# State and output products of an attention tile gathered around the next tile's transposes and scores

## The chip, the cores and the metric

The kernel runs on one core of a Trainium2 chip. The metric is the device time of one execution in microseconds (us); three executions of the kernel before took 817.29 to 818.46 us, with a median of 818.1 us. In the text PE is the matrix engine (TensorE), DVE the vector engine, ACT the scalar engine, POOL the GpSimd engine, SP the queue engine that issues transfers. PEld is the loading of weights into PE.

## The reference

Three layers follow each other on 3072 tokens (4 batches of 768, 384 features):

```python
for t in range(S):                      # linear attention, 8 heads of 48, decay w
    cur = einsum('bhd,bhe->bhde', u[None] * kt, vt)
    y[:, :, t] = einsum('bhd,bhde->bhe', rt, state + cur)
    state = wt[:, :, :, None] * state + einsum('bhd,bhe->bhde', kt, vt)
x = y.transpose(0, 2, 1, 3).reshape(B * S, H * D)
h = x @ w_in                            # dense layer, 384 -> 2048 -> 384
x = (max(h, 0) + alpha * min(h, 0)) @ w_out
expert_idx = argmax(cosine(x, expert_emb) / tau)
out = gate * (relu(x @ w1[expert_idx]) @ w2[expert_idx])   # one of 8 experts, 384 -> 1024 -> 384
```

All is in float32.

## The kernel before, in words

**Attention** is cut into 24 tiles: six chunks of 128 steps in time for each of four batches (`n // 4` is the chunk, `n % 4` the batch). A tile's loaded data (`ld`, 1348.5 KB, two buffers) is worked on in parts that the code calls by a digit and a letter for the engine. The parts that matter here:

- 0D and 1D (lines 277 to 290): two scans on DVE that turn the decays into running products, and products with k. 6D (line 302): r times the running product on DVE, and the old state scaled into `sbd` on POOL. 7D: the term with `u` (a reduction and a product on DVE, giving `dv`). 8A: a check of the decays on ACT.
- 2P, 2A: k is transposed on PE (`kt_ps`, four products, L341) and copied by ACT into the single buffer `Kt`.
- 3P, 3A: the scores of all eight heads (`a_ps`, two PSUM tiles, eight products that the trace shows as 16 matmuls, L352), copied by ACT into the single buffer `A` and masked by POOL.
- 9P, 9A: the new part of the state, `Kt` times v (`u_ps`, L368), added to `sbd` on DVE (L376). It is called from inside 4P and 4D.
- 4P, 4D: the output y of the tile, from the old state (L391) and from the scores (L394) into `y_ps`, then `dv` is added on DVE (L400).
- 5P, 5A, 5D: y is transposed (`t_ps`, L409) and split into `xh` and `xl`, the input of the dense layer.

The matrices that PE uses differ in shape: `kt`, `t` and all products of the dense layer use the whole array (128*128 in the trace), the scores use half of its rows (64*128), the state and y use half of its columns (128*64; `u` shows 48 of 64 active).

**The dense layer** works on blocks of three tiles (`BLK`, eight blocks, 384 tokens). Block j has 16 steps `f`; step T = 16 j + f computes `l1` (nine products into `h_ps`, L453; ACT, DVE, ACT and DVE then make `gh` and `gl` from it) and `l2` of the step two before (nine products into three `o_ps`, L488). Every value is split into a high and a low part, hence three products for one. After a block, `route` finds each token's expert with some 60 small DVE operations, a few of them after each step.

**The order** is written out by hand. For the first block it is the string `PLAN`; from then on the table `sched` gives for each step T the parts of tiles that run in it. Parts 2 to 5 come at a step's start (before `l1` on PE), parts 0, 1, 6, 8, 9 and 7 at its end (after `l2`). For a tile n of block q the start is `16 * (q - 1) + AT[3][n - B0[q]]`, and `LAGS` says how many steps later each part comes:

```python
LAGS = [0, 1, 4, 4, 6, 7, 2]
AT = {2: [-1, 6], 3: [-4, 1, 7]}
```

So a tile's transposes and scores stand together at one step, its state and y two steps later, its transposed y one step after that: three groups on PE for each tile, each between the `l2` of one step and the `l1` of the next. `run` (line 942) also issues the load of tile n + 2 when every part that reads tile n is recorded. PSUM holds three `o` buffers, two `h` buffers and three `a` buffers; `a` is shared by `kt_ps`, both `a_ps`, `u_ps`, `y_ps`, `t_ps` and a small product of `route`.

**The expert layer** follows from about 557 us on; its weights are loaded by index and its order is another table.

Of the kernel before, what the change touches and what calls it, by code (L numbers as in the profile page):

```python
# [8 lines left out]
F32 = mybir.dt.float32  # L9
# [8 lines left out]
B, H, S, D = 4, 8, 768, 48  # L18
# [3 lines left out]
NCH = S // CH  # L22
NTILE = B * NCH
HP = H // 2
# [6 lines left out]
BLK = [3] * 8  # L31
NB = len(BLK)
B0 = [sum(BLK[:j]) for j in range(NB)]
# [25 lines left out]
STEP7 = 5  # L59
# [12 lines left out]
START = [-8, -6, -5]  # L72
LAGS0 = [0, 1, 2, 2, 3, 4, 1]
LAGS1 = [0, 1, 4, 4, 6, 7, 2]
LAGS = [0, 1, 4, 4, 6, 7, 2]

LOADS = [(0, "w"), (0, "rk"), "id", "v", (0, "n"), "e", (1, "w"), (1, "rk"), (1, "n"), (2, "w"), (2, "rk"), (2, "n"), 0, 1, 2, 3, "u"]
PLAN = """
# [11 lines left out]
m.15 p1P.6 p1A.6 4P.5 4D.5 o.12 5P.5 5A.5 d.14 p0P.7 o.13 p0A.7 c2.15 5D.5 p1P.7 c3.15 n.15 p1A.7  # L90
"""

AT1 = {1: [0, 4, 8], 2: [0, 4, 8]}
AT = {2: [-1, 6], 3: [-4, 1, 7]}
NSG = 4
WP = 1536
W_MID = 0.95
# [9 lines left out]
def tile_main(ctx, tc, keep, x2d, tbl, att, w_in, w_out, alpha, u_row, u_col, emb, tau, w1, w2, cst, out):  # L107
# [13 lines left out]
    ps_h = ctx.enter_context(tc.tile_pool(name="ps_h", bufs=2, space=bass.MemoryType.PSUM))  # L121
    ps_a = ctx.enter_context(tc.tile_pool(name="ps_a", bufs=3, space=bass.MemoryType.PSUM))
# [57 lines left out]
    def rT(n, i):  # L180
        return ld_t[n][:, i * HP * CH:(i + 1) * HP * CH].rearrange("p (h t) -> p h t", h=HP)

    def nat(n, i):
        return ld_t[n][:, LN + i * DM:LN + (i + 1) * DM]
# [43 lines left out]
    wt_t, tmp = {}, {}  # L228
# [132 lines left out]

    def att_9P(n):
        v = nat(n, 2)
        up = tmp["u", n] = ps_a.tile([128, HP, D], F32, tag="a", name="u_ps")
        for h in range(H):
            i = h % 2
            q = slice(64 * i, 64 * i + D)
            PE.matmul(out=up[q, h // 2, :], lhsT=Kt[:, h // 2, q], rhs=v[:, D * h:D * h + D], start=True, stop=True)  # L368
# [11 lines left out]
    def att_4P(n):  # L380
        c, b = divmod(n, B)
        r, v = rT(n, 0), nat(n, 2)
        A = tmp.pop(("A", n))
        if 0 < c < NCH - 1:
            att_9P(n)
        yp = tmp["y", n] = ps_o.tile([128, DM], F32, tag="o", name="y_ps") if n < BT else ps_a.tile([128, DM], F32, tag="a", name="y_ps")

        for hp in range(HP):
            for q in (slice(0, 64), slice(64, 128)):
                if c:  # L390
                    PE.matmul(out=yp[q, 2 * D * hp:2 * D * (hp + 1)], lhsT=r[:, hp, q], rhs=sbd[n % 2][:, hp, :], start=(hp == 0), stop=False)  # L391
            for h in (2 * hp, 2 * hp + 1):
                for q in (slice(0, 64), slice(64, 128)):
                    PE.matmul(out=yp[q, D * h:D * h + D], lhsT=A[:, HP * (h % 2) + h // 2, q], rhs=v[:, D * h:D * h + D], start=(c == 0 and h == 0), stop=(h == H - 1))  # L394
# [31 lines left out]
    def parts(q, n):  # L426
        if q == 2 and n // B == NCH - 1 or q == 9 and n > BT:
            return []
        if q == 7:
            return [p for p in PART[7] if n in ND and (p != "7D" or n not in AD) or n not in ND and p == "7D"]  # L430
        return PART[q]
# [423 lines left out]
    if True:  # L855
# [40 lines left out]
        for n in range(B0[NB - 1], NTILE):  # L896
            c, b = divmod(n, B)
            t0 = b * S + c * CH
            SP.dma_start(out=x2d[t0:t0 + CH, :], in_=sbd_all.rearrange("p i h d -> p (i h d)")[:, 0:ROW])


        sched = {}
        for n in range(NTILE):
            j = max(q for q in range(NB) if B0[q] <= n)
            t0 = START[n] if j == 0 else 16 * (j - 1) + (AT1[j] if j < 3 else AT[BLK[j]])[n - B0[j]]
            for q, d in enumerate(LAGS0 if j == 0 else LAGS1 if j == 1 else LAGS):
                sched.setdefault(t0 + d, []).append((q, n))
            sched.setdefault({1: 0, 2: 1}.get(n, t0 + 3), []).append((8, n))
        sched.setdefault(1, []).append((2, 2))
# [3 lines left out]
        ran = set()  # L913
# [25 lines left out]
        def run(name, *a):  # L939
            if name == "w":  # L940
                return warm(*a)
            if (name, *a) in ran:
                return
            ran.add((name, *a))
            FN[name](*a)
            if name[0].isdigit() and a[0] != 2 and int(name[0]) in READ:
                n = a[0]
                m = n + 3 if n < 2 else n + 2
                if m < NTILE and m not in ld_t and all((p, n) in ran for q in READ for p in parts(q, n)):
                    load_att(m)  # L950

        def flush():
            for k in sorted(k for k in m_t if k[0] == 0):
                run("h", k[1])
                run("d", k[1])

        def pieces(T, qs):
            for q, n in sched.get(T, []):
                if q in qs:
                    for p in chain(parts(q, n), parts(7, n) if q == 6 else []):  # L960
                        run(p, n)

        def convs(T, late):
# [37 lines left out]
        def step(k):  # L1001
            for r in list(bg):
                for _ in range(k):
                    q = next(r, DONE)
                    if q == DONE:
                        bg.remove(r)
                    elif q == DONE_T:
                        state["known"] = len(KIND)
                    if q:
                        break  # L1010
# [4 lines left out]
        for T in range(16 * NB + 2):  # L1015
            j, f = divmod(T, 16)
            flush()
            pieces(T, (2, 3, 4, 5))
            convs(T, 0)
            if j < NB:  # L1020
                if j:
                    l1(j, f)
                else:
                    for p in "lmn":
                        run(p, f)
            for i, d in enumerate(WPD):
                c = T + OFF - d
                if c % 2 and 0 <= c < 2 * NG:
                    run(f"p{i}P", c // 2)
                    run(f"p{i}A", c // 2)  # L1030
            if T == 16 * (NB - 1):
                xg.extend(atp.tile([128, 2, ROW], F32, tag=t, name="xg") for t in ("st", "st", "at"))
                for t in xg:
                    POOL.memset(t, 0.0)
            if T >= 2:
                run("o", T - 2) if T < 18 else l2((T - 2) // 16, (T - 2) % 16)
                if (T - 2) % 16 == 15:
                    o_evac((T - 2) // 16)
                    q = (T - 2) // 16
                    bg.append(chain(route(q), *((early_table(), early_loads()) if q == NB - 2 else (last_table(),) if q == NB - 1 else ())))  # L1040
            convs(T, 1)
            pieces(T, (0, 1, 6, 8, 9))
            if j and (j, f) in m_t:
                l1_lo(j, f)
            step(STEP7 if j >= NB - 1 else 1)
            if T == 32:
                zero = sgp.tile([128, DM], F32, tag="sg", name="zero")
                POOL.memset(zero, 0.0)
            if 32 <= T < 32 + NTILE:
                SP.dma_start(out=out[(T - 32) * CH:(T - 31) * CH, :], in_=zero)  # L1050
            for fn, i, at in EARLY:
                if T - 16 * NB == at:
                    (split, x_T)[fn](0, i)
# [31 lines left out]
        n = len(STEPS)  # L1085
# [318 lines left out]
```

## Time and profile before

| what | value |
|---|---|
| median of three executions | 818.1 us (817.29 to 818.46) |
| the profiled execution | 816.11 us, its span 814.0 us |
| PE busy | 792.5 us, 97% of the span |
| PE weight loads | 752.3 us |
| DVE, ACT, POOL busy | 582.6, 439.4, 302.7 us |
| HBM traffic | 141 GB/s over the span |
| granted PE clock | 0.998 |

The profile's page gives busy times of engines; the timeline gives start and duration of each instruction on an engine, with equal instructions that follow each other merged into one row with a count. Matmuls overlap in a pipeline, so the step from one row's start to the next row's start is what a row costs, not its duration.

### The profile page before, as it was taken

The numbers are of one execution on the slowest core, as the hardware profiler recorded it, in microseconds if no ns is written. First come the engines' busy times: TensorE is split into PE (matmuls) and PEld (weight loads), VectorE is DVE, ScalarE is ACT, GpSimd is POOL, SyncE is SP. The second block draws the span as 40 slices with busy tenths as digits, with TensorE's granted clock in tenths as the row PEclk, the third lists the DMA queues.
The fourth block names the chain that finished last, engine by engine and source line by source line (L and its number), as shares of the span: only waits on it lengthen the run. The fifth ranks groups of instructions, "written<-read, shape, count | busy, mean of one in ns | idle before, by whom it ended". The sixth has DMA issues, their size and how long they took to land. (4 is left out here: it accounts for less than half of the span.)

```text
span 814.0 us, 16574 instructions
## 1 busy us (share of the span) xinstructions
PE 792.5 (97%) x6500; PEld 752.3 (92%) x6500; DVE 582.6 (72%) x1226; ACT 439.4 (54%) x885; POOL 302.7 (37%) x365
## 2 busy tenths in 40 slices
PE   9989999999999999999999999997999999999997
PEld 5778899999999999999999999896899999999997
DVE  7998867877676676686586574728987677768672
ACT  5897644445335345435435444326557676767662
POOL 2202032232232223224124112154466776767731
PEclk9999999999999999999999999999999999999999
DMA  9565311224334222113103100064756787786750
GB/s 323 191 208 165 148 69 33 106 99 137 127 132 132 80 72 95 69 31 101 71 35 108 60 31 1 31 251 143 180 199 217 266 289 245 222 283 211 262 188 33
DMA packets 31622, 114.85 MB, mean 141 GB/s; under 512 B 5756, under 2 KB 13148, under 8 KB 29232
## 3 DMA queue, kind: packets, MB, share of 16 engines
q0 software_dynamic: 13952, 59.86, 22.5%
q1 hardware_dynamic: 17584, 53.85, 19.3%
q8 instruction: 53, 0.87, 0.5%
q14 instruction: 33, 0.27, 0.2%
HBM read 99.36 MB, written 15.51 MB: 141 GB/s over the span
## 5 line engine op out<-in xcount | busy, mean ns | idle before, releaser
L463 ACT ACTIVATE m<-h_ps,al_sb 128x384 f32<-128x384 f32 x128 | 74.2, 580 | 133.6 <-PE h_ps L453 130.5
L467 DVE TENSOR_TENSOR m<-h_ps,m 128x384 f32<-128x384 f32 x128 | 70.9, 554 | 91.6 <-ACT m L463 89.2
L473 ACT ACTIVATE gh<-m 128x384 fp32r<-128x384 f32 x128 | 67.1, 525 | 102.5 <-DVE m L467 98.0
L360 POOL TENSOR_SCALAR_AFFINE_SELECT A<-A 128x512 f32<-128x512 f32 x48 | 34.5, 743 | 200.9 <-ACT A L359 200.9
L478 DVE TENSOR_TENSOR gl<-m,gh 128x384 fp32r<-128x384 f32 x128 | 81.8, 641 | 34.6 <-ACT gh L473 33.3
L741 POOL DMA_INDIRECT raw<-in_w,wix x64 | 67.9, 1061 | 50.6 <-DVE w0l L753 23.2
L783 PE MATMUL h_ps<-yh,w0h 128*128 128x256 f32 x264 | 77.2, 292 | 4.0 <-DVE g2l L788 3.9
L783 PE MATMUL h_ps<-yl,w0h 128*128 128x256 f32 x264 | 74.6, 283 | 0.9 <-DVE yl L774 0.9
L783 PE MATMUL h_ps<-yh,w0l 128*128 128x256 f32 x264 | 74.2, 281 | 0.0
L753 DVE TENSOR_TENSOR w1l<-raw,w1h 128x768 fp32r<-128x768 f32 x64 | 60.6, 953 | 18.5 <-ACT w1h L752 14.7
L453 PE MATMUL h_ps<-xh,win1h 128*128 128x384 f32 x192 | 68.2, 355 | 2.4 <-DVE m L467 2.4
L453 PE MATMUL h_ps<-xh,win0h 128*128 128x384 f32 x192 | 68.7, 358 | 1.5 <-DVE m L467 1.5
L753 DVE TENSOR_TENSOR w0l<-raw,w0h 128x768 fp32r<-128x768 f32 x64 | 60.7, 958 | 12.3 <-ACT w0h L752 11.3
L488 PE MATMUL o_ps<-wout0h,gl 128*128 128x392 f32 x192 | 65.5, 341 | 0.5 <-DVE gl L478 0.5
L488 PE MATMUL o_ps<-wout0h,gh 128*128 128x392 f32 x192 | 65.8, 343 | 0.0
L488 PE MATMUL o_ps<-wout1h,gh 128*128 128x392 f32 x192 | 65.7, 342 | 0.1
L488 PE MATMUL o_ps<-wout1h,gl 128*128 128x392 f32 x192 | 65.5, 341 | 0.0
L488 PE MATMUL o_ps<-wout0l,gh 128*128 128x392 f32 x192 | 65.4, 340 | 0.0
L488 PE MATMUL o_ps<-wout1l,gh 128*128 128x392 f32 x192 | 65.2, 340 | 0.0
L453 PE MATMUL h_ps<-xh,win1l 128*128 128x384 f32 x192 | 65.0, 339 | 0.2 <-DVE win1l L225 0.2
L453 PE MATMUL h_ps<-xl,win0h 128*128 128x384 f32 x192 | 64.9, 338 | 0.0
L453 PE MATMUL h_ps<-xl,win1h 128*128 128x384 f32 x192 | 64.8, 338 | 0.0
(281 smaller groups left out, 2266.4 us busy)
## 6 DMA issues: line engine op xcount, KB each, us to landing
ld<-in_att SPq DMA_DIRECT2D x18, 1348.5 KB
stg<-in_w_in SPq DMA_DIRECT2D x24, 256.0 KB
stg<-in_w_out SPq DMA_DIRECT2D x8, 768.0 KB
x2d<-rows SPq DMA_DIRECT2D x24, 194.0 KB
out<-zero SPq DMA_DIRECT2D x24, 192.0 KB
ld<-in_att SPq DMA_DIRECT2D x5, 512.0 KB
ld<-in_att SPq DMA_DIRECT2D x3, 452.5 KB
raw<-in_w,wix POOLq DMA_INDIRECT x64
```

Of the source, the lines that this page charges most:

```text
L360: POOL.affine_select(out=h, in_=h, pattern=[[0, HP], [1, CH]], compare_op=ALU.is_gt, fill=0.0, base=0, channel_multiplier=-1)
L453: PE.matmul(out=h, lhsT=w[:, k, :], rhs=x[:, k, :], start=(n == 0), stop=(n == 3 * KD - 1))
L463: ACT.activation(out=m, in_=h_t[j, f], func=AF.Copy, scale=al_sb[:, f:f + 1])
L467: DVE.tensor_tensor(out=m, in0=h_t.pop((j, f)), in1=m, op=ALU.min)
L473: ACT.activation(out=gh, in_=m_t[j, f], func=AF.Copy)
L478: DVE.tensor_tensor(out=gl, in0=m_t.pop((j, f)), in1=gh.bitcast(F32), op=ALU.subtract)
L488: PE.matmul(out=o_t[j][i], lhsT=g[:, s], rhs=w, start=(f == 0 and n == 0), stop=(f == KF - 1 and n == 2))
L741: POOL.indirect_dma_start(out=t, out_offset=None, in_=src, in_offset=idx(wix[:, h, COL[s]:COL[s] + 1]))
L753: DVE.tensor_tensor(out=lo, in0=a, in1=hi.bitcast(F32), op=ALU.subtract)
L783: PE.matmul(out=h, lhsT=w[:, k, :], rhs=x[:, k, :], start=(n == 0), stop=(n == 3 * KD - 1))
```

## The change

From tile 6 on (the first of block 2) each tile has one group on PE, at step 5, 10 or 15 of the block before (`AT`, `at_y`). `tile_group` records it: u of tile n, kt of tile n + 1, y of tile n, scores of tile n + 1, transposed y of tile n. `u_ps` of these tiles takes an `h` buffer instead of an `a` buffer. The DVE parts of a tile now lie around the group of the tile before: 0D three steps ahead of it, 1D two, 6D one, 8A at it, 7 one after. Tile 6, with no such group before it, has its kt and scores alone one step before its own group. `route` makes no step ahead of a group and two steps after one. In the last chunk (tiles 20 to 23) there is no state and no kt, as before.

```diff
-LAGS = [0, 1, 4, 4, 6, 7, 2]
+LAGS = {0: -3, 1: -2, 6: -1, 8: 0, 7: 1}
...
-AT1 = {1: [0, 4, 8], 2: [0, 4, 8]}
-AT = {2: [-1, 6], 3: [-4, 1, 7]}
+AT1 = [0, 4, 8]
+AT = [5, 10, 15]
...
     def att_9P(n):
-        up = tmp["u", n] = ps_a.tile([128, HP, D], F32, tag="a", name="u_ps")
+        up = tmp["u", n] = ps_h.tile([128, HP, D], F32, tag="h", name="u_ps") if n in at_y else ps_a.tile([128, HP, D], F32, tag="a", name="u_ps")
...
     def att_4P(n):
-        if 0 < c < NCH - 1:
+        if 0 < c < NCH - 1 and ("9P", n) not in ran:
             att_9P(n)
...
         sched = {}
+        at_y = {n: 16 * (q - 1) + AT[n - B0[q]] for q in range(2, NB) for n in range(B0[q], B0[q] + BLK[q])}
         for n in range(NTILE):
-            j = max(q for q in range(NB) if B0[q] <= n)
-            t0 = START[n] if j == 0 else 16 * (j - 1) + (AT1[j] if j < 3 else AT[BLK[j]])[n - B0[j]]
-            for q, d in enumerate(LAGS0 if j == 0 else LAGS1 if j == 1 else LAGS):
+            if n in at_y:
+                t = at_y[n - 1] if n - 1 in at_y else at_y[n] - 2
+                for q, d in LAGS.items():
+                    sched.setdefault(t + d, []).append((q, n))
+                sched.setdefault(at_y[n], []).append((4, n))
+                if n - 1 not in at_y:
+                    sched.setdefault(t + 1, []).extend([(2, n), (3, n)])
+                continue
+            t0 = START[n] if n < B0[1] else AT1[n - B0[1]]
+            for q, d in enumerate(LAGS0 if n < B0[1] else LAGS1):
                 sched.setdefault(t0 + d, []).append((q, n))
...
+        def tile_group(n):
+            m, more = n + 1, n // B < NCH - 1
+            nxt = parts(2, m) if m < NTILE else []
+            if more:
+                run("9P", n)
+            if nxt:
+                run("2P", m)
+            if more:
+                run("9A", n)
+            if nxt:
+                run("2A", m)
+            run("4P", n)
+            run("4D", n)
+            if m < NTILE:
+                run("3P", m)
+                run("3A", m)
+            for p in parts(5, n):
+                run(p, n)
...
-            pieces(T, (0, 1, 6, 8, 9))
+            pieces(T, (0, 1, 6, 7, 8, 9))
...
-            step(STEP7 if j >= NB - 1 else 1)
+            step(STEP7 if j >= NB - 1 else 0 if T + 1 in at_y.values() else 2 if T - 1 in at_y.values() else 1)
```

The first place is PE, the state and y of a tile in the middle (`o_ps` and `h_ps` are the dense layer). Before:

```order
L368 MATMUL u_ps<-ld,Kt 48x48 x8
L391 MATMUL y_ps<-sbd,ld 64x96 x2
L394 MATMUL y_ps<-ld,A 64x48 x4
...
L453 MATMUL h_ps<-xh,win0h 128x384
L453 MATMUL h_ps<-xl,win0h 128x384
```

The rows of y stand four times there, which the line of dots leaves out. With the change:

```order
L488 MATMUL o_ps<-wout0h,gl 128x392
L368 MATMUL u_ps<-ld,Kt 48x48 x8
L341 MATMUL kt_ps<-ident,ld 128x128 x4
L391 MATMUL y_ps<-sbd,ld 64x96 x2
L394 MATMUL y_ps<-ld,A 64x48 x4
...
L352 MATMUL a_ps<-ld 128x128 x8
L409 MATMUL t_ps<-ident,y 128x128 x3
L453 MATMUL h_ps<-xh,win1h 128x384
```

The next tile's transposes came between u and y, its scores between y and its transposes; y is again four pairs of rows.

The second place is PE at the last tile, 23. With the change:

```order
L488 MATMUL o_ps<-wout1h,gl 128x392
L391 MATMUL y_ps<-sbd,ld 64x96 x2
L394 MATMUL y_ps<-ld,A 64x48 x4
...
L409 MATMUL t_ps<-ident,y 128x128 x3
L453 MATMUL h_ps<-xh,win1h 128x384
```

Here no scores stand between y and the transposes that read it; before, a step's 18 products of the dense layer stood there.

The third place is DVE around the y of a tile in the middle. Before:

```order
L285 TENSOR_TENSOR ld<-ld,PS 128x512
L478 TENSOR_TENSOR gl<-m,gh 128x384
L376 TENSOR_TENSOR st<-u_ps,sbd 48x192 x2
L400 TENSOR_TENSOR y<-y_ps,dv 128x384
L467 TENSOR_TENSOR m<-h_ps,m 128x384
L288 SCALAR_TENSOR_TENSOR PS<-ld,anew 128x519
```

With the change:

```order
L467 TENSOR_TENSOR m<-h_ps,m 128x384
L304 TENSOR_TENSOR ld<-ld,PS 128x512
L478 TENSOR_TENSOR gl<-m,gh 128x384
L376 TENSOR_TENSOR st<-u_ps,sbd 48x192 x2
L400 TENSOR_TENSOR y<-y_ps,dv 128x384
L421 TENSOR_TENSOR xl<-t_ps,xh 128x3x128
L467 TENSOR_TENSOR m<-h_ps,m 128x384
```

The low part of the transposed y (L421) follows y at once, the other work of the tile is a step or more away, and nothing of `route` stands between `gl` and the state.

## Rows read from the trace of the kernel before

**Rows 1.** Stretches: us, PE, PEld, DVE, ACT, POOL busy, clock, DMA, GB/s.
```profile
120.00:512.00 392.00, 391.91 (x3286) 379.39 (x3285) 274.37 (x656) 173.90 (x363) 108.89 (x147) 1.00 0.24 79
```

**Rows 2.** Timeline of PE, transposes and scores of a tile: start, duration, line, tiles.
```profile
329.06 0.34 PE L488 MATMUL o_ps<-wout0h,gl 128*128 128x392 f32 x1
329.24 0.60 PE L341 MATMUL kt_ps<-ident,ld 128*128 128x128 f32 x4
329.77 1.16 PE L352 MATMUL a_ps<-ld 64*128 64x128 f32 x16
...
331.14 0.34 PE L453 MATMUL h_ps<-xl,win0h 128*128 128x384 f32 x1
```

**Rows 3.** Timeline of PE, state and y of a tile.
```profile
337.17 0.34 PE L488 MATMUL o_ps<-wout0h,gl 128*128 128x392 f32 x1
337.44 0.56 PE L368 MATMUL u_ps<-ld,Kt 128*48 128x48 f32 x16
337.84 0.35 PE L391 MATMUL y_ps<-sbd,ld 128*64 128x96 f32 x4
...
339.21 0.39 PE L394 MATMUL y_ps<-ld,A 128*64 128x48 f32 x8
339.53 0.44 PE L453 MATMUL h_ps<-xh,win0h 128*128 128x384 f32 x1
339.81 0.34 PE L453 MATMUL h_ps<-xl,win0h 128*128 128x384 f32 x1
```

**Rows 4.** Timeline of PE, transposed y of a tile.
```profile
342.66 0.34 PE L488 MATMUL o_ps<-wout0h,gl 128*128 128x392 f32 x1
342.84 0.49 PE L409 MATMUL t_ps<-ident,y 128*128 128x128 f32 x3
...
343.35 0.34 PE L453 MATMUL h_ps<-xl,win1h 128*128 128x384 f32 x1
```

**Rows 5.** Timeline of PE, the one place where kt follows u.
```profile
47.41 0.56 PE L368 MATMUL u_ps<-att,Kt 128*48 128x48 f32 x16
47.91 0.66 PE L341 MATMUL kt_ps<-ident,ld 128*128 128x128 f32 x4
48.40 0.88 PE L244 MATMUL wt_ps<-ident,stg 128*128 128x128 f32 x6
```

**Rows 6.** Timeline of PE, the one place where scores follow y.
```profile
24.67 1.25 PE L394 MATMUL y_ps<-ld,A 128*64 128x48 f32 x32
25.84 1.16 PE L352 MATMUL a_ps<-att 64*128 64x128 f32 x16
26.94 0.50 PE L439 MATMUL idle<-oneb 128*128 128x384 bf16 x2
```

**Rows 7.** Timeline of PE, last chunk: scores alone, and y without a state.
```profile
436.14 0.34 PE L488 MATMUL o_ps<-wout1h,gl 128*128 128x392 f32 x1
...
437.78 0.34 PE L453 MATMUL h_ps<-xl,win0h 128*128 128x384 f32 x1
...
463.27 0.34 PE L488 MATMUL o_ps<-wout0h,gl 128*128 128x392 f32 x1
...
465.54 0.34 PE L453 MATMUL h_ps<-xl,win0h 128*128 128x384 f32 x1
```

**Rows 8.** Timeline of DVE, state and y of the tile of rows 3.
```profile
338.71 0.74 DVE L376 TENSOR_TENSOR st<-u_ps,sbd 48x192 f32<-48x192 f32 x2
339.65 0.56 DVE L400 TENSOR_TENSOR y<-y_ps,dv 128x384 f32<-128x384 f32 x1 [0.20 <-PE y_ps L394]
```

**Rows 9.** Timeline of PE and DVE, the one transposed y that waits for its y.
```profile
159.45 0.34 PE L488 MATMUL o_ps<-wout1h,gl 128*128 128x392 f32 x1
159.88 0.55 PE L409 MATMUL t_ps<-ident,y 128*128 128x128 f32 x3
...
159.27 0.56 DVE L400 TENSOR_TENSOR y<-y_ps,dv 128x384 f32<-128x384 f32 x1
```

**Rows 10.** Busy times in the stretch of one tile's load (columns of rows 1).
```profile
319.00:326.00 7.00, 7.00 (x51) 6.91 (x46) 6.22 (x13) 3.32 (x9) 0.95 (x2) 1.00 0.55 200
```

More of the change, by code (lines that the diff above doesn't have):

```diff
@@ L959, in pieces @@
                 if q in qs:
-                    for p in chain(parts(q, n), parts(7, n) if q == 6 else []):
+                    if q == 4 and n in at_y:
+                        tile_group(n)
+                        continue
+                    for p in chain(parts(q, n), parts(7, n) if q == 6 and n not in at_y else []):
                         run(p, n)
```

## The prediction, made before the changed kernel ran

> **What bounds the kernel now.** I read the busy times by stretch first. Between 120 and 512 us, where the dense layer and nearly all changed tiles lie, PE is busy for 391.91 of 392 us, while DVE is busy for 274.37 and ACT for 173.90 [rows 1]. PE waits for practically nothing there, so the time of this stretch is the sum of what its instructions cost on PE, and an engine beside it matters only where the change makes PE wait. Then I read PE's timeline around one tile, start by start. A product of the dense layer costs 0.18 us (0.177, read over many): the start of a transposed y follows the last one at that distance [rows 4]. What an attention group costs is then the time from the last dense product before it to the second one behind it, less 0.18 for each of the two; the second, because the first one after a group can be late too.
>
> **What the three groups cost now.** Transposes and scores: 329.06 to 331.14, 2.08 us [rows 2]. State and y: 337.17 to 339.81, 2.64 us [rows 3]. Transposed y: 342.66 to 343.35, 0.69 us [rows 4]. Together 5.41 less six times 0.18, so 4.33 us for a tile. Part of it are joints between products of different array shape. The transposed y has none: 0.51 us from its start to the second dense product, less 0.18, is 0.11 for each of three [rows 4]. Four kt would be 0.44 and take 0.53 where scores follow, 0.09 more [rows 2]. Entering u takes 0.27 instead of 0.18, and the first dense product after y takes 0.28 instead of 0.18 [rows 3]. Between u and y, which use the same shape, there is no extra.
>
> **What one group will cost.** The order on PE is u, kt, y, scores, transposed y. I lay it together from places where the same neighbours occur in this trace.
> - Into u: 0.27 [rows 3].
> - u until kt starts: 0.50, where u until y takes 0.40 [rows 5, 3].
> - kt after u: 0.49, 0.05 over the bare 0.44 [rows 5]; half the array's shape follows, which adds the 0.09 seen before the scores [rows 2]: 0.58.
> - y, its exit to another shape included: 1.69 [rows 3]. That an exit to scores is no dearer than one to a dense product is seen once: y's row ends at 25.92 and the scores start at 25.84, 0.08 before that [rows 6]; the dense product starts 0.07 before the end of y's row (339.60) [rows 3].
> - Scores: 331.14 less 0.28 less 329.77, 1.09 [rows 2]; after y 1.10 [rows 6].
> - Transposed y until the second dense product: 0.51 plus the 0.05 that kt pays after u, 0.56 [rows 4, 5]. Transposes after scores do not occur in the steady part; bounds are 0 and the 0.10 of a dense product after y, and kt after u is the nearest row because it is the same kind of product.
>
> The sum is 4.69 less 0.36, 4.33 us: **for a tile in the middle nothing is gained**. Two groups fewer save one way into u's shape and the ways back to the dense layer, but kt now splits u from y, two products of one shape that had no joint between them. This holds for tiles 6 to 18.
>
> The Trainium skill speaks against the change here: its page TensorEngine Tiling (Array Packing), Tiling Modes, Key Properties, says that a change of the tiling mode, not of the tile alone, drains TensorE. By that rule, at one price for every change of shape, the group with five changes would be dearer than the three groups with four; it is the second rival below. The free joint from u to y agrees with it, the unequal joints above (0.05 to 0.10 on each side) do not.
>
> **The last chunk.** Tiles 20 to 23 have no state and no kt. Scores alone cost 436.14 to 437.78, 1.64; y alone 463.27 to 465.54, 2.27 [rows 7]. With the transposed y that is 1.64 + 2.27 + 0.69 less 1.08, 3.52. In one group: 2.27 less the exit of 0.28, then 1.09, then 0.56, less 0.36: 3.28. So 0.24 is saved for each of tiles 20 to 22, and the same for tile 19, which has u but no kt: 4 x 0.24, 1.0 us.
>
> **Tile 23** ends with y and then its transposes, with nothing in between. DVE must first add dv. From y's end on PE to DVE's start 0.05, the operation 0.56 [rows 3, 8], from its end (159.83) to a waiting transpose 0.05 [rows 9]; y's row ends 0.07 after the next instruction could have started. That is a wait of 0.73. Without it the tile would save 0.05 (2.27 + 0.69 less 0.72 is 2.24, against 1.99 + 0.56 less 0.36). So +0.68.
>
> **A wait that goes.** One transposed y (tile 7) waits now: it starts 0.43 after the last dense product, instead of 0.18 [rows 9]. In the new group 1.09 us of scores lie between y and its transposes, and DVE needs 0.73: it would not wait. -0.25.
>
> **What else moves, and why I put it at nothing.**
> - 17 of the 18 groups have these 0.36 us of slack (1.09 less 0.73), if DVE is free when y ends. y ends on PE 2.84 us into the group (0.50 + 0.58 + 1.69 + 0.07). On DVE the state sums (0.74 for both [rows 8]) stand ahead of it, and ahead of them `gl` of the step before; so `gl` may end as late as 2.1 us into the group, and it belongs to an `l1` that ended nine dense products, 1.6 us, before the group began. `route` was cleared from just there.
> - Buffers: the second scores tile takes the buffer that kt leaves; ACT has the 1.69 us of y to copy it. u now takes an `h` buffer, left by the `l1` two steps back.
> - Scans, r times P and the term with u go to steps with no group; DVE has 118 of 392 us free [rows 1]. If that cover fails, `gl` comes late and `l2` waits; it has more than a step (3.2 us) of lead.
> - POOL's masks and sums keep their count; the scores are masked 16 us before they are read.
> - The load of tile n + 2 still follows y of tile n on SP, but its first scan now comes two steps after the group: about 1.4 us of the group, 2 x 3.19 and 1.6 of `l1`, 9.4 us. One load, 1.38 MB, lies within a stretch of 7 us (200 GB/s x 7 us is 1.40 MB [rows 10]). It fits by 2.4 us. Zeroing and row writes change places with it on SP; they are not near the end of anything. If a load were late by more, the scan would hold DVE, and PE a step later.
>
> **Sum:** -1.0 + 0.68 - 0.25, about -0.6 us. The profiled execution took 816.11 us, 2.0 below the median of 818.1; against the median I predict **817.5 us**. That is less than 0.2% of the time (1.6 us), about the least that a measurement of this kernel can tell from no change.
>
> **Rivals.**
> 1. *The joints inside a group are free.* Only kt to y and scores to transposes were not seen as such. At nothing they would save 0.09 in 13 tiles and 0.05 + 0.10 (a scores exit as dear as that of y) in 17: 1.2 + 2.6 = 3.8 us, so 813.7. For it: u to y is free. Against: the joints of rows 5 and 6 were paid in full. Chance 0.10.
> 2. *Every change of shape costs the same*, slower than before. A tile's 4.33 us hold 0.73 of joints: 3.60 is bare (kt 0.44, scores 0.89, u 0.36, y 1.59, transposed y 0.33; u, scores and y stripped of the 0.04, 0.2 and 0.1 at their ends). Four changes, so 0.18 each. A group in the middle has five, one more in 13 tiles: +2.4; tiles 19 to 22 have three instead of four: -0.7; with tile 23 (+0.7) and the wait that goes (-0.25) +2.1, so 820.2. It decides from 0.15 us for the pair of joints around kt beyond what rows 2 and 5 show. Chance 0.12.
> 3. *DVE comes to y late in every group.* It decides where y starts on DVE more than 0.36 us after PE has finished it: each 0.1 beyond costs 1.7 us over 17 tiles. If a 0.56 operation stands in front, 0.2 x 17 = 3.4, so 817.5 + 3.4 = 820.9. For it: now DVE did come late once [rows 9]. Against: the cleared order. Chance 0.08.
>
> **How the numbers follow.** The sum as forecast has 0.65; 0.05 is left for a late load or something unseen. Within the forecast, bounds of the two unseen joints and of the slack give about 1 us either way, so that 0.10 of its 0.65 falls below 816.5. Faster: 0.10 + 0.10 = 0.20. Slower: 0.12 + 0.08 = 0.20, the unseen included in the middle. Same: 0.60. The range takes in rival 2 and the forecast's spread, and leaves out most of rivals 1 and 3: 815.0 to 820.4.
>
> **What would show it.** In the new trace a middle group should take 4.69 us from the last dense product before it to the second behind it; kt 0.50 after u, y 0.58 after kt, scores 1.69 after y, transposes 1.09 after scores. Tile 23's transposes should start some 0.7 us late and wait for DVE's y. Wrong would be: PE gaps before transposes in the other groups, a scan that waits for a transfer, or a group of 4.5 or 4.9 us.

## The result and the profile after

Five executions of the changed kernel took 821.55 to 823.7 us, median 822.73; five of the kernel before, beside them, 817.29 to 819.0, median 818.46. The ratio, which is taken over all the runs and not from the two medians, is 1.0055 with an interval of 1.004 to 1.0069: **slower by 0.55%, 4.3 us**. The forecast was 817.5, its range ended at 820.4.

The profiled execution took 823.7 us (span 822.0), 7.6 us more than that of before. The attention part accounts for 4.8 of it: one step of the dense layer starts at 121.01 us before and at 121.84 now, a step near the end of that part at 499.59 and 505.26. The rest lies outside the changed part. It is two stretches at a lower clock, and the time from the last matrix product to the end, 5.9 us before and 8.0 now, which lies anywhere from 5.8 to 8.0 in later runs of both kernels and their variants. Busy times by stretch (columns of [rows 1]):

```profile
43.00:47.00 4.00, 4.00 (x60) 3.54 (x61) 3.96 (x6) 3.87 (x14) 0.00 (x0) 0.57 0.69 244
569.00:573.00 4.00, 4.00 (x20) 4.00 (x19) 3.62 (x16) 0.64 (x3) 0.71 (x1) 0.57 0.23 95
...
120.00:517.00 397.00, 392.88 (x3287) 379.84 (x3286) 275.72 (x654) 173.59 (x364) 105.07 (x148) 1.00 0.26 78
```

The first two rows are the stretches at a lower clock: each holds 3.4 us at 0.50, the lower of the two levels (1.2 instead of 2.4 GHz), and 0.57 is the mean of the row. Shortly before, PE had stood for 1.2 us (until 42.15) and for 2.1 us (until 568.65). Twelve of the fourteen profiles of this document have the first stretch and eleven the second, variants of both kernels among them; the first profile of before has neither. The third answers to [rows 1]. PE does as much work as before (392.88 us against 391.91) and stands for 4.1 us, where it stood for 0.1. So the loss is waiting, not work.

**The group on PE** came out as laid together. Timeline of PE around a tile in the middle (start, duration, line, tiles), answering to [rows 2 to 4]:

```profile
331.26 0.34 PE L488 MATMUL o_ps<-wout0h,gl 128*128 128x392 f32 x1
331.53 0.56 PE L368 MATMUL u_ps<-ld,Kt 128*48 128x48 f32 x16
332.03 0.66 PE L341 MATMUL kt_ps<-ident,ld 128*128 128x128 f32 x4
332.61 0.39 PE L391 MATMUL y_ps<-sbd,ld 128*64 128x96 f32 x4
...
334.34 1.16 PE L352 MATMUL a_ps<-ld 64*128 64x128 f32 x16
335.43 0.55 PE L409 MATMUL t_ps<-ident,y 128*128 128x128 f32 x3
...
336.00 0.34 PE L453 MATMUL h_ps<-xl,win0h 128*128 128x384 f32 x1
```

From 331.26 to 336.00 it is 4.74 us, 4.38 without the two dense products, against a forecast of 4.33 and 4.33 before. In the last chunk (answering to [rows 7]) a group is 3.65, so 3.29 against the forecast of 3.28:

```profile
458.81 0.34 PE L488 MATMUL o_ps<-wout0h,gl 128*128 128x392 f32 x1
...
462.46 0.34 PE L453 MATMUL h_ps<-xl,win0h 128*128 128x384 f32 x1
```

**The new waits.** The view of waits gives for PE between 115 and 515 us (engine, line, what it waited for: us in total, times, longest), where before had no row at all:

```profile
PE o_ps L488 <- DVE rows L496: 2.0, 2, 1.8
PE t_ps L409 <- DVE y L400: 1.2, 3, 0.7
PE rk_ps L559 <- DVE s_pre L548: 0.8, 2, 0.6
```

The first is the largest. After a block `o_evac` copies three finished tiles out of PSUM into `rows` (L496, L498), and `route` writes those rows to `x2d` (L572). The next block's copy uses the same buffer, so it must wait until the writes have landed. The view of line 572 says who waited for the writes to land (us, times); in before the list was empty:

```profile
  DVE rows L496: 5.7, 4
  ACT rows L498: 3.2, 2
```

One such place, by the timelines of SP (transfers issued), POOL, DVE and PE:

```profile
169.30 0.34 SPq L572 DMA_DIRECT2D x2d<-rows  x1
179.04 0.33 SPq L178 DMA_DIRECT2D ld<-in_att  x1
179.41 1.78 SPq L572 DMA_DIRECT2D x2d<-rows  x2
...
182.24 1.16 POOL L575 DMA_INDIRECT tbl<-tokid,s_pi  x1 [0.17 <-DVE xl L421]
183.70 0.97 POOL L575 DMA_INDIRECT tbl<-tokid,s_pi  x1 [0.18 <-issue]
184.98 0.97 POOL L575 DMA_INDIRECT tbl<-tokid,s_pi  x1 [0.19 <-issue]
...
192.65 0.57 DVE L496 COPY rows<-o_ps 128x392 f32<-128x392 f32 x1 [2.97 <-DMA x2d<-rows]
...
193.37 0.42 PE L488 MATMUL o_ps<-wout0h,gh 128*128 128x392 f32 x1 [1.75 <-DVE rows L496]
```

The first row write goes out at 169.3. The other two stand on SP behind the next tile's load, which waits for the last reader of its buffer, and go out at 179.4 and 179.9. Then POOL issues three table writes (scattered, one small element for each token). By its completion events the last row write landed at 192.6, 12.7 us after its issue; the first one took 1.9. DVE starts its copy at once, and PE, which needs the PSUM tiles, 0.7 us after that.

In before the same transfers stood beside each other, only earlier (timelines of SP, POOL and DVE):

```profile
174.63 0.91 SPq L572 DMA_DIRECT2D x2d<-rows  x2
...
175.79 1.17 POOL L575 DMA_INDIRECT tbl<-tokid,s_pi  x1 [3.21 <-DVE s_pi L567]
...
188.68 0.56 DVE L496 COPY rows<-o_ps 128x392 f32<-128x392 f32 x1
```

The last row write, issued at 175.1, stood behind a load, had table writes beside it and took 12.5 us here as well, but the copy came 13.6 us after it. Over the first five blocks, the time from the issue of a block's last row write to the end of the last product that the copy reads was 13.5 to 16.2 us in before and is 9.1 to 10.1 now; the landing took 7.5 to 12.5 us and now takes 7.3 to 12.7. So the landing is about as slow as it was, and the time allowed for it is 3 to 7 us shorter.

The third of PE's waits, the small product `rk` of `route`, by the timelines of DVE, POOL and PE:

```profile
233.77 1.00 DVE L545 TENSOR_TENSOR s_oh<-ivals,rows 128x24 bf16<-128x24 f32 x1
234.69 0.16 DVE L548 CAST s_pre<-carry 128x8 bf16<-128x8 f32 x1
234.88 0.95 DVE L549 TENSOR_TENSOR carry<-carry,s_oh 128x8 f32<-128x8 f32 x1
...
233.65 1.08 POOL L298 TENSOR_TENSOR ld<-ld 128x384 f32<-128x384 f32 x1 [5.83 <-DMA ld<-in_att]
234.81 1.00 POOL L299 TENSOR_TENSOR ld<-ld,u_sb 128x384 f32<-128x384 f32 x1
...
236.50 0.17 PE L559 MATMUL rk_ps<-s_pre,oneb 128*128 128x24 bf16 x1 [0.63 <-DVE s_pre L548]
```

Two DVE operations on 24 and 8 numbers a row take 1.00 and 0.95 us while POOL multiplies r, k and u. Their median over the stretch is 0.18 and 0.17. Both have two inputs in SBUF. (The CAST between them keeps its 0.16, but it falls into the change from one product to the next.) A reduction with one input that ran wholly beside such a product kept its median of 0.54:

```profile
186.33 1.02 POOL L298 TENSOR_TENSOR ld<-ld 128x384 f32<-128x384 f32 x1
...
186.42 0.54 DVE L333 TENSOR_REDUCE dg<-ld 128x8 f32<-128x384 f32 x1
```

**The bookkeeping**, from starts of dense products, PE's time against before: 13 middle groups +0.6 (0.05 each); four groups of the last chunk -0.9; tile 23's transposes, which wait for y, +0.65; tile 7's wait that went -0.3; the copies of rows +2.3 (1.9 at 193 us, 0.4 at 388); `rk` +1.1 (0.8 and 0.3); DVE late in three groups +1.3 (0.45, 0.75, 0.1). Sum 4.8, what the two traces differ by in this part.

### The profile page after: what moved, and what is told of

Same layout as the page of the kernel before. It is cut to its first block, busy times and chain, and to the rows that moved or that the text cites. A ratio compares the mean times of both kernels' runs of the same rounds, so it can differ in the third digit from the quotient of the medians.

```text
span 822.0 us, 16591 instructions
## 1 busy us (share of the span) xinstructions
PE 796.5 (97%) x6500; PEld 755.4 (92%) x6500; DVE 583.4 (71%) x1226; ACT 439.0 (53%) x885; POOL 297.8 (36%) x365
## 4 chain that ended last, share of the span: by engine, by line
PE 70%; DVE 13%; issue 6%; DMA 4%; ACT 4%; POOL 1%; SPq 1%; another core or an unknown queue 0%; POOLq 0%; DVEq 0%; ACTq 0%
PE h_ps L453 19%; PE o_ps L488 19%; PE h_ps L783 9%; PE o_ps L809 8%; DMA x2d<-rows 3%; PE o_ps L841 2%; PE h_ps L819 2%; PE a_ps L352 2%; PE y_ps L394 2%; PE y_ps L391 2%; DMA stg<-in_w_in 1%; DVE gl L478 1%; DVE m L467 1%; PE t_ps L409 1%; DVE stg L211 1%
## 5 line engine op out<-in xcount | busy, mean ns | idle before, releaser
L478 DVE TENSOR_TENSOR gl<-m,gh 128x384 fp32r<-128x384 f32 x128 | 78.8, 618 | 22.3 <-ACT gh L473 20.9
L453 PE MATMUL h_ps<-xh,win0h 128*128 128x384 f32 x192 | 66.8, 348 | 1.5 <-DVE m L467 1.5
L453 PE MATMUL h_ps<-xh,win0l 128*128 128x384 f32 x192 | 65.3, 340 | 0.0
## 6 DMA issues: line engine op xcount, KB each, us to landing
ld<-in_att SPq DMA_DIRECT2D x18, 1348.5 KB
```

What stands on the lines that cost most here:

```text
L453: PE.matmul(out=h, lhsT=w[:, k, :], rhs=x[:, k, :], start=(n == 0), stop=(n == 3 * KD - 1))
L478: DVE.tensor_tensor(out=gl, in0=m_t.pop((j, f)), in1=gh.bitcast(F32), op=ALU.subtract)
```

## The experiments

Ratios are against the kernel before, run beside each; its median moved between 816.3 and 820.5 us from one set of runs to another, so times of different sets are compared by their ratios. A line of dots in an edit stands for lines left out. The first four were made with the place of the row writes behind the load as the suspect.

**The pace of `route`, even again.** Edit:

```diff
-            step(STEP7 if j >= NB - 1 else 0 if T + 1 in at_y.values() else 2 if T - 1 in at_y.values() else 1)
+            step(STEP7 if j >= NB - 1 else 1)
```

> The changed kernel with route's old pace: one step of it after every step T, none skipped ahead of a group, none doubled behind it. Theory (route's pace pushed its small product on PE to within 0.9 us of the DVE operations that feed it, and two of a block's three row writes behind a waiting load): the waits of the small product go (about 1.1 us in the changed kernel: 0.78 and 0.33), the wait of the rows copy (2.3 us: 1.93 and 0.46) shrinks but need not go, since one row write still stands behind a load; in exchange the seven small operations that make the one-hot rows now stand on DVE ahead of a group's y, and the transposes of up to two groups a block wait 0.2 to 0.4 us more. Sum: 1 to 3 us faster than the changed kernel's 822.7, so 820 to 822. Rival (the loss sits in the joints of the group, not in route): no change, 822.7.

Measured 839.86 us, ratio 1.0228 (1.0199 to 1.0257): far slower than any theory had it. The view of line 572 (waits, and the time from issue to landing, min/median/max, where all completions are recorded):

```profile
  DVE rows L496: 17.5, 5
  ACT rows L498: 14.6, 5
...
DMA to landing us min/median/max: 2.2/2.4/11.5
```

Two of a block's row writes now go before the load and land in 2.4 us; the third stands behind the load, and a table write was issued even before that load; it lands 11.5 to 18.0 us after its issue (at the longest the load itself took 15.6). The copy comes due (the last product that it reads ends) 10.6 us after that issue in each of the five blocks. `rk` does not wait at all here. So the new pace had not caused the loss from the rows but held part of it off; for `rk` it is the other way round. A wait also costs more than its length. These are stretches of this run (us, busy times of the engines, granted clock of PE third from the end):

```profile
188.00:199.00 11.00, 4.38 (x26) 4.09 (x24) 2.07 (x5) 1.87 (x4) 1.98 (x2) 0.81 1.02 138
199.00:205.00 6.00, 6.00 (x19) 6.00 (x20) 3.79 (x8) 2.85 (x9) 1.36 (x2) 0.50 0.02 7
```

PE stood for 6.6 us; while it stood, its clock fell to 0.50, the lower of its two levels (1.2 instead of 2.4 GHz), and the next step of 18 products took 5.96 us instead of 3.18.

**Loads a step later**, so that all row writes go out ahead of them. Edit (the loads are collected in a list and recorded at the end of the next step):

```diff
+        loads, now = [], [0]
...
-                    load_att(m)
+                    (loads.append((m, now[0])) if now[0] >= 20 else load_att(m))
...
+            now[0] = T
...
+            while loads and loads[0][1] < T:
+                load_att(loads.pop(0)[0])
```

> The changed kernel with the load of tile n + 2 recorded one step later, so that on SP the three row writes of a block stand ahead of it instead of behind it; nothing else differs. Theory (the rows copy waited because two row writes were queued behind a load that itself waited some 8 us for PE to finish a tile): no wait of the rows copy is left, minus 2.0 to 2.4 us, so about 820.5. Rival (the write itself is slow because of the zeroing writes behind it): the wait stays, 822.7. Rival (loads now land late for their scan): slower than 822.7, with DVE waiting for a load.

Measured 821.06, ratio 1.0005 (0.9985 to 1.0025): 0.5% below the changed kernel's ratio. All fifteen row writes of the first five blocks landed in 2.1 to 2.8 us and nobody waited for them. This supports the suspicion, but it moves three things: the writes no longer follow a load, they land before the table writes start, and they go out 17 to 19 us ahead of the copy.

**kt before u** in the group, so that u and y, of one shape, follow each other:

```diff
-            if more:
-                run("9P", n)
             if nxt:
                 run("2P", m)
             if more:
+                run("9P", n)
                 run("9A", n)
```

> The changed kernel with one swap inside the group: kt of the next tile first, then u, y, scores, transposes, so that kt stands next to the dense layer's whole-array products and u next to y. By the joints read off the trace (whole array to u 0.13, u to kt 0.16, kt to y 0.09 against kt 0, into u 0.13, u to y 0) a middle group falls from 4.37 to 4.12 us, 13 times: minus 3.2 us, so about 819.5; where y now comes 0.25 us sooner and DVE is late, transposes may wait some tenths of that back. Rival (only the number of groups counts, not the order inside): no change, 822.7.

Measured 821.75, ratio 1.0024 (0.9996 to 1.0051), 2.5 us below the changed kernel by the ratios, in runs that spread from 816.9 to 833.4. A step with a middle group took 7.28 us instead of 7.56 in its trace: 0.28 for each of 13, 3.6 us. (Joint by joint, from a later run's group below: 0.10 at the entry, 0.10 between u and y, 0.05 at kt, 0.04 within y.) The profiled execution, 833.4 us, is well above the median of its run: three copies waited 11.1 us for row writes that took up to 15.6 us. So in that execution the loss from the rows was larger than in the changed kernel's profile; the 0.28 us a step came out again in the faster versions below (7.26 to 7.30).

**Tile 23's transposes behind the next `l1`:**

```diff
         h_t[j, f] = h
+        if (j, f) == (NB - 2, KF - 1):
+            for p in PART[5]:
+                FN[p](NTILE - 1)
...
-            for p in parts(5, n):
-                run(p, n)
+            if n < NTILE - 1:
+                for p in parts(5, n):
+                    run(p, n)
```

> The changed kernel with the transposes of the last tile's y moved from right behind y to behind the nine dense products of the same step; nothing else differs. Theory (those transposes wait for DVE's y, 0.73 us predicted, 0.65 read): minus 0.6 to 0.7 us, so about 822.1. Rival (the wait hides one that would come right after, at the copies of the new block's input): no change or slower, with a wait of the next step's first product.

Measured 825.62, ratio 1.0056 (1.0031 to 1.008): not told from the changed kernel. In the trace the tile's step took 5.35 instead of 6.10, so the 0.65 to 0.75 us are gained where they were expected, and lie below what the time can tell.

**The row writes in ACT's queue.** Is it SP's order that delays them?

```diff
-            SP.dma_start(out=x2d[t0:t0 + CH, :], in_=rows[:, i, 0:ROW])
+            ACT.dma_start(out=x2d[t0:t0 + CH, :], in_=rows[:, i, 0:ROW])
```

> The changed kernel, with the row writes of a block issued by ACT instead of SP: the loads stay where they are, only the queue in which the writes stand is another. Theory (a row write that stands behind a load on SP's queue lands too late for the copy of the next block's rows): the waits of DVE and ACT for x2d<-rows before their copies are below 0.5 us in sum over all blocks, and the time is 2 to 4 us below the changed kernel, 818.5 to 820.5. Rival (the copies wait because the load takes the DMA engines, whichever queue the writes stand in): the waits stay at 2 us or more, the time at 822 to 823.

Measured 867.34, ratio 1.0578 (1.0556 to 1.06). The theory of the queue falls. View of line 572, and the timeline of ACT at one block:

```profile
  DVE rows L496: 39.8, 5
  ACT rows L498: 36.9, 5
```

```profile
264.65 0.34 ACTq L572 DMA_DIRECT2D x2d<-rows  x1
...
280.86 0.89 ACT L498 ACTIVATE rows<-o_ps 128x392 f32<-128x392 f32 x2 [12.51 <-DMA x2d<-rows]
```

ACT issues a write only where its program stands, so the last one of the first block goes out at 186.9 instead of 179.9, and in all five blocks the copy comes due 3.5 us after the last write, instead of 9 to 10. The one shown lands 16.1 us after its issue, although no load stands in its queue and the last load had landed at 264.0. Another, at 344.0, goes out 2.0 us after the landing of the load before it and takes 8.6. What was in flight beside both are table writes, issued at 260.3 to 262.9 and at 339.6 to 342.2. So neither SP's queue nor a load is needed for a row write to land late, and the rival of the expectation, the load's use of the DMA engines, does not explain it either. The size of this run's loss comes from both, late landings and less time for them.

**The kernel before, with loads and row writes two steps later:**

```diff
-HOLD = [1, 2, 1]
+HOLD = [3, 2, 1]
...
+            while loads and loads[0][1] < T - 1:
+                load_att(loads.pop(0)[0])
             pieces(T, (0, 1, 6, 8, 9))
```

> The kernel before, its order on PE untouched, with the load of a tile recorded two steps later and the rows' routing held back two steps, so that all row writes of a block stand behind a load and are issued some 10.5 us before the copy of the next block's rows (before: 17; changed kernel: 11 to 13). Theory (the change lost its time to this place of the writes, not to the groups on PE): DVE and ACT wait for x2d<-rows, PE stands for 1 us or more in at least one block, and the time is 1 to 8 us above before. Rival (the waits come from what the one group does to DVE and PE): no such wait, the time within 0.5 us of before.

Measured 830.14, ratio 1.0114 (1.0095 to 1.0133), 9.3 us, with every group on PE as in before. So row writes that land late cost microseconds without any regrouping. But five of the six blocks had no wait; their margin came out at 14 to 18 us instead of the 10.5 meant, and behind a load their writes landed in 6 to 8. Nearly all of the loss came from one block, in which the last row write stood on SP behind a zeroing write and went out at 187.5, among table writes of 185.4, 187.3 and 190.6, long after the load had landed (180.8) and 2.3 us before the end of the last product that the copy reads. It took 9.9. DVE's copy and PE there:

```profile
197.48 0.57 DVE L496 COPY rows<-o_ps 128x392 f32<-128x392 f32 x1 [8.07 <-DMA x2d<-rows]
```

```profile
198.19 0.42 PE L488 MATMUL o_ps<-wout0h,gh 128*128 128x392 f32 x1 [4.55 <-issue]
```

**The table writes later**, which separates the two suspects: the row writes stay behind the load. (`table` is a new function that holds the lines of the table write.)

```diff
             SP.dma_start(out=x2d[t0:t0 + CH, :], in_=rows[:, i, 0:ROW])
             yield
+            if j < NB - 2:
+                continue
...
+        if j < NB - 2:
+            yield WAIT
+            yield WAIT
+            for i in range(nb):
+                table(B0[j] + i, i, pi)
+                yield
```

> The changed kernel with the three table writes of a block (POOL, tbl<-tokid) issued after all its row writes and two steps more; the row writes stay behind the load on SP. In the changed kernel a row write alone landed 2 us after its issue, behind a load 6 to 8, and behind a load with table writes beside it 10 to 13. Theory (the table writes beside them are what makes the row writes late; a place behind the load alone costs 5 us, which the copy does not feel): row writes land within 8.5 us, DVE and ACT wait less than 0.3 us for x2d<-rows in all, and the time is 1.5 to 4 us below the changed kernel. Rival (the place behind the load decides): the waits stay at 2 us or more, and the time within 1 us of the changed kernel's.

Measured 817.13, ratio 1.0013 (0.9997 to 1.003), 3.4 us below the changed kernel by the ratios. Line 572 has no waiter any more:

```profile
DMA to landing us min/median/max: 2.1/6.6/8.2
```

Behind the load a row write now lands in 6.3 to 8.2 us, 1.3 to 1.9 us before the copy comes due, so the copy does not feel it. The theory of the table writes holds, with a limit: a block's first table write still goes out 1.1 to 2.3 us behind its last row write, and only the second and third go out when the row write has landed or is within 0.8 us of it. So one table write beside a row write does no harm here; it takes two or three.

**The same edit in the kernel before, and a second profile of before:**

> The kernel before with the table writes of a block issued after its row writes and two steps more, nothing else. Theory (before loses at most 1.3 us to late row writes, in one block in some executions, so the 3.4 us that this edit gives the changed kernel are the change's own loss): within 0.2% of before, ratio 0.998 to 1.000. Rival (the edit is a gain of its own, whatever the order of the groups): ratio 0.994 to 0.997, as it gives the changed kernel.

> The kernel before, unchanged, for a second profile of it. All theories: no wait of PE over 0.45 us between 125 and 510 us, every step without attention at 3.18 to 3.19 us. Open is the part behind 590 us: from the start of the dense product at 587.4 us to the end the first profile took 226.6 us; the changed kernel's (from 593.3) and the one with late loads' (from 589.8) took 228.7. If the change lengthens that part, this run shows 226.6 again; if it is the spread of executions, it shows up to 228.7.

With the edit before takes 815.16, ratio 0.9981 (0.9969 to 0.9993): a small gain there too, 1.6 us; no table write runs beside the row writes of its first five blocks, and the last of each lands in 5.5 to 8.1 us. The second profile of before (819.85 us) shows where a part of the gain can lie, in its waits of DVE, and it shows a stretch at a lower clock at the same place as the changed kernel:

```profile
DVE rows L496 <- DMA x2d<-rows: 0.8, 1, 0.8
```

```profile
43.00:47.00 4.00, 4.00 (x67) 3.52 (x67) 3.93 (x6) 3.36 (x12) 0.00 (x0) 0.77 0.77 282
```

One copy waits there for a row write that took 14.4 us, and the step is 1.0 us longer; all its other steps between 125 and 510 us are as in the first profile. Its last part took as long as in the first, 5.9 us from the last product to the end. So of the 3.4 us some 1.6 are a loss that before has as well, in some executions; the change's own part is about 2 us. Each of these ratios has an interval of 1.0 to 1.3 us either way, so the split is rough.

**Without the u term.** POOL's two products L298 and L299 are left out for tiles 6 to 23:

```diff
     def att_u(n):
+        if n >= 6:
+            return
```

> The changed kernel without the two POOL products for the term with u (L298, L299) of tiles 6 to 23, so that term is left out of the result. Theory (DVE's operations stretch while POOL runs these two: gl 1.36 instead of 0.55, s_oh 1.00 instead of 0.17, so that the small product of the routing waits for s_pre): no gl longer than 0.9 and no s_oh longer than 0.3 us between 125 and 510 us, the waits of PE for s_pre below 0.1, the late DVE in the step at 285 us smaller; 1.5 to 2 us less on PE. Rival (DVE is late there because of its own order: dv, gl and the small operations in one step): the same waits, 0.8 us for s_pre, within 0.5 us.

Measured 820.75, ratio 1.0041 (1.0016 to 1.0066), 1.1 us below the changed kernel by the ratios (the intervals overlap), with 0.7 us of waits for rows still in it. The view by line of `gl` and of `carry` (count, duration in ns min/median/max), first the changed kernel, then this one:

```profile
L478 DVE TENSOR_TENSOR gl<-m,gh x96: 529/557/1374, 125.2 to 507.3; 128x384 fp32r<-128x384 f32 x96
...
L549 DVE TENSOR_TENSOR carry<-carry,s_oh x18: 166/167/954, 167.8 to 490.3; 128x8 f32<-128x8 f32 x18
```

```profile
L480 DVE TENSOR_TENSOR gl<-m,gh x97: 526/558/871, 125.2 to 507.4; 128x384 fp32r<-128x384 f32 x97
...
L551 DVE TENSOR_TENSOR carry<-carry,s_oh x18: 167/168/169, 170.8 to 490.4; 128x8 f32<-128x8 f32 x18
```

No `gl` is longer than 0.87, no small operation longer than 0.23, `rk` does not wait, and the late group at 285 us is gone: 1.9 us less on PE (1.1 and 0.8), as expected; a step at 457 us is 0.24 longer. The late groups at 133 us (tile 6, 0.45) and at 415 us (tile 19, 0.1) stay, so those are not POOL's doing.

**Versions that beat both.** First the loads a step later, kt before u, tile 23 as above, and `rk` a step later (`HOLD = [2, 2, 1]`); then the same with the table writes later.

> The changed kernel with four edits: loads recorded a step later (row writes ahead of them), kt before u in the group, the last tile's transposes behind the next dense layer's products, and the small product of the routing held back a step more. Theory (the change itself gains 1.0 in the last chunk; kt first saves 0.28 in 13 groups, 3.6; the row waits, rk's 1.1 and the last tile's 0.65 go): 1.0 + 3.6 below before, less about 1.5 of groups in which DVE is late: 3 us below before, ratio 0.996. Rival (the time goes to spread and to something not yet seen): within 1 us of before.

> The version of the run with four edits (loads a step later, kt before u, last tile's transposes behind the next products, rk a step later) and the table writes two steps behind the row writes as well. Theory: all row writes already land in 2 to 3 us there, so the table writes cost nothing more; the gain of that run stays, ratio to before 0.995 to 0.998. Rival (table writes also stretch the loads that follow them, and late loads bring POOL's products onto DVE's small operations): loads land in under 7.5 us, the late groups at 216 and 280 us go, ratio 0.993 to 0.995. Third: the table writes now stand in front of the next load and make it later, ratio above 0.998.

Measured 817.98, ratio 0.9971 (0.9958 to 0.9985), and 812.5, ratio 0.996 (0.9946 to 0.9973): both faster than before, the second by 3.3 us; their intervals overlap, so the table writes' part there is not told apart. Of the second, the landing of the row writes and a group on PE:

```profile
DMA to landing us min/median/max: 2.0/2.5/2.9
```

```profile
326.75 0.34 PE L491 MATMUL o_ps<-wout0h,gl 128*128 128x392 f32 x1
326.92 0.60 PE L341 MATMUL kt_ps<-ident,ld 128*128 128x128 f32 x4
327.45 0.56 PE L368 MATMUL u_ps<-ld,Kt 128*48 128x48 f32 x16
327.85 0.35 PE L391 MATMUL y_ps<-sbd,ld 128*64 128x96 f32 x4
...
331.19 0.34 PE L453 MATMUL h_ps<-xl,win0h 128*128 128x384 f32 x1
```

4.44 us from 326.75 to 331.19, 0.30 less than in the changed kernel. The late group at 281 us is still there (1.2 us over the median), and loads still took up to 8.7 us: the rival that the table writes made those late falls.

## Why the prediction was wrong

- **The group on PE, nothing gained:** right. Its terms were 0.27, 0.50, 0.58, 1.69, 1.09 and 0.56; measured 0.27, 0.50, 0.58, 1.73, 1.09 and 0.57. Of the 0.05 too little, 0.04 lies in y's first products behind kt (0.22 us from the first row to the second, 0.18 behind u), not in y's exit; over 13 tiles it makes 0.6 us.
- **Last chunk, tile 23, tile 7:** right. -0.9 for -1.0, +0.65 for +0.68, -0.3 for -0.25. With the 0.6 above, PE's own account comes to about 0 instead of -0.6.
- **"Zeroing and row writes change places with it on SP; they are not near the end of anything":** this is the step that failed. A row write is what the next block's copy waits for, and that copy is what PE's next block waits for. [rows 1 to 10] hold none of it: where nothing waits, the view of waits shows nothing, and I did not look up how much time lay between landing and copy. In the first block of before it was 1.0 us (landing at 187.65, copy at 188.68). What the change did was to take 3 to 7 us from the time between a block's last row write and the copy, which now waits in four blocks, 5.7 us in all on DVE and 2.3 on PE. The experiments with the table writes and with the late loads put 3.4 to 4 us on these waits, about 2 of them new with the change.
- **"`route` was cleared from just there" and POOL's "count":** failed as well. POOL's products for u kept their count but now wait for the load (5.83 us in the row at 233.65) and fall together with the two pieces of `route` that follow a group. The small operations stretch from 0.17 to 1 us, and 1.9 us of PE are lost; the run without the products shows it.
- **17 groups with slack for DVE's y:** 14 had it. One failed beside POOL's products (0.75, gone in the run without them); tile 6 (0.45) and tile 19 (0.1) failed without them too.
- **The rivals.** Free joints: no, each was paid. Every change of shape at one price: 820.2 came nearer to 822.7 than the forecast, but by luck, for the loss lay elsewhere; at 0.18 each the group would have been 4.51, and it is 4.38. The rule on tiling modes in the Trainium skill (TensorEngine Tiling (Array Packing), Tiling Modes, Key Properties) is not contradicted by that, since kt first does give back 0.28 to 0.30 by putting u and y together; only its price is not one price. DVE late in every group: three of 18.

In one sentence: the change moved no work off PE, and beside PE it shortened the time between a block's row writes, slow to land in both kernels, and the copy that waits for them, and brought POOL's products together with `route`.

## What to carry to other kernels

Where an edit is forecast to gain nothing on the bound engine, what remains to be asked is which buffers are freed late: for every transfer whose place changes, find who reuses its source, and how long before that it lands now, also where no wait shows. A write's landing time is not a constant: look at what other writes are in flight beside it, in any queue. And when small DVE operations stand on a path, look up where POOL's elementwise work falls, not only how much of it there is.

## What the runs showed of the hardware that was not expected

- A row write of 194 KB landed in 1.9 to 3.2 us alone (between 160 and 500 us). The last one of a block took 5.5 to 8.1 us behind a 1348.5 KB load with no table write in flight (before with the table writes later), 6.8 to 8.2 with one (the changed kernel with them later), and 7.3 to 18.0 with two or three, in either kernel; in ACT's queue 7.5 to 16.1. In the changed kernel the packets of the last write of the first block had all moved by 186.2 us; its last completion came at 192.6. The Trainium skill, DMA: Bandwidth & Descriptors, Queues, rings and completion order, says that a semaphore increment lands only after every earlier write of that DMA engine, across its queues; the run with ACT's queue and the one with the table writes later agree with that, but do not prove it to be the cause. Why a table write itself takes 4 to 17 us to land was not examined.
- DVE operations with two inputs in SBUF lasted up to 0.8 us longer when POOL was already running a product from SBUF (0.55 to 1.36 for `gl`, 0.17 to 1.00 for `s_oh`), whatever their size. The reduction L333, with one input, did not (0.54), but one TENSOR_SCALAR with one input did (L537, 0.17 to 0.99 at 296.0 us). The Trainium skill, SBUF — State Buffer, Who interferes with whom, says that a DVE instruction with two SBUF inputs contends with a GpSimd instruction that reads SBUF; the rows at 233.65 to 234.88 agree.
- PE's clock fell to 0.50 (1.2 GHz) while PE stood for 6.6 us, and the next step cost 5.96 us instead of 3.18: the wait was paid 1.4 times.
